# Reordering flips, w transposes and token-mix matmuls in four slots of a retention + phase-MLP kernel

## The chip, the cores and the metric

One core of one Trainium2 chip. The metric is device microseconds of one execution, lower is better. A run is called slow when it is over 1.5% above the fastest run of the same kernel, and fast otherwise.

## The reference, cut to what matters

```python
# retention over q, k, v (4 batches, 8 heads, 768 positions, 64 wide)
state = gamma * state + k_t (x) v_t ;   y_t = scale * q_t @ state
x = y as (4, 768, 512)
# phase MLP
theta = x @ w_theta
zr, zi = x * cos(theta), x * sin(theta)
y = w_tok_r @ zr + w_tok_i @ zi          # mixes the 768 positions
u = x + y
out = u + relu(u @ w_ch)
```

## The kernel before

The retention works in twelve pairs of 128-row blocks, three pairs to a batch. The kernel is scheduled by hand: one slot for each pair, numbered n = 0 to 11 in the code, and called first to twelfth here. In slot n it finishes pair n-1, does most of pair n, prepares pair n+1, loads pair n+3 and mixes some row tiles of the MLP. The order of the calls is the order on every engine. The parts that the change touches:

```python
def prep(n, name, engines):   # cast k, or scale q and v, to bf16 (raw loads are f32)
    ...
def flip(n, name):            # 8 TensorE transposes into a PSUM tile of ring "tr"
    ps = psum.tile([P, 2, NP, P], BF, name="kq_ps", tag="tr", bufs=2)
    ...
    copy(t, ps)               # VectorE, to kqT
def zmul(n, a):               # VectorE: z = (cos, sin) * x
def moe_M(m, lo, hi):         # token mix of row tile m over chunks lo..hi of z; needs wT and z
def moe_u(m):                 # VectorE: u = y + x; frees the PSUM bank of y
def moe_O(m):                 # 4 matmuls u @ w_ch, into ring "tr" too
def moe_out(m):               # VectorE: relu + add; frees that PSUM tile
def w_tok(t0):                # 2 x 6 transposes of w rows, into ring "tr" twice;
                              # copied by VectorE (real) and ScalarE (imaginary)
```

The ring "tr" has two buffers. Every flip, w transpose, transpose of u or of x and output matmul takes the next one in turn and waits until its last reader is done.

In the profile lines below, L183 with kq_ps is a flip, L340 with y_ps a token mix (M), L368 with o_ps an output matmul (O), L393 with w_ps a w transpose, L312 with th_ps a theta matmul, L208 with at_ps the scores and L231 with yT_ps the retention's Y. kqb is a cast k, q or v, and wtr the real part of the transposed w. PE is TensorE and PEld its weight loads, DVE is VectorE, ACT ScalarE, POOL GpSimd, and SPq the queue that issues the DMAs.

```python
# third slot (n = 2), after the first half's mask
    zmul(1, 0)
    ret_A(2, 1)
    ret_mask(2, 1)
    ret_Y(2, 0); ret_I(2, 0); ret_I(2, 1)
    moe_M(0, 2, 3)
    ret_Y(2, 1)
    ret_out(2, 0, AC.copy)
    zmul(1, 1)
    ret_out(2, 1, DV.tensor_copy)
    w_tok(1)
    prep(3, "k", (PL,))
    moe_M(0, 3, 4)
    flip(3, "k")
    ...
# fourth slot and on (nG = 3): n = 3, 4, 5, ...
        if nxt and n > nG + 1: preps(PP)               # q and v of pair n+1, on GpSimd
        ...                                            # theta of pair n-1
        if nxt and nG + 2 < n + 1 < limit: flip(n + 1, name)
        if n == nG + 1 or ...: moe_M(first, 2, 4)
        ...                                            # state, second half of the scores, Y
        if n < U_DMA: moe_U(done)                      # u transposes, copied by ScalarE
        if n in (nG, nG + 1):
            prep(n + 1, "k", (AC,)); preps(DP); flip(n + 1, "k")
        if n == nG or ...: moe_M(first, 2, 4)
        if n in (nG, nG + 1): flip(n + 1, "q")
        if not two:
            moe_M(first, 4, nT); moe_u(first)
            if n < nG + 3: w_tok(n - nG + 3)
        ...
        for t in done: moe_O(t); moe_out(t)
```

## Time and profile before

| | before |
|---|---|
| timed runs | 175.59, 175.73, 175.74 us |
| profiled run | 174.05 us (span 172.3) |
| TensorE busy | 155.0 us, 90% of the span |
| TensorE waiting between 27 and 75 us | 7.9 us in all the waits |
| end of the last matmul | 169.1 us |

The page's second part shows where TensorE is not full. Each digit is its busy share in one fortieth of the span, in tenths:

```profile
PE   7679887799589689899999999999999999999992
```

From the eighteenth digit on TensorE is full. The loose part is the first 75 us, and the change works there.

### The profile page before, as it was taken

What the parts mean: (1) busy time and instruction counts of PE and PEld (TensorE: products, weight loads), DVE (VectorE), ACT (ScalarE), POOL (GpSimd) and SP (SyncE); (2) the same over time, 40 slices, a digit from 0 to 9 for tenths busy, and PEclk for the clock granted to TensorE, in tenths of its full rate; (3) what the DMA queues carried; (4) which work ended last, traced back from release to release, by engine and by line L of the source; (5) the groups of instructions that cost most, each with busy time, mean ns of one, the idle gap of its engine ahead of it and who ended that gap; (6) DMA issues with size and microseconds to landing.
All of it is one profiled execution on the core that took longest, in us unless ns stands there. A gap on an engine that the chain in (4) does not pass through costs nothing.

```text
span 172.3 us, 4658 instructions
## 1 busy us (share of the span) xinstructions
PE 155.0 (90%) x1949; PEld 88.3 (51%) x1975; DVE 104.5 (61%) x138; ACT 81.1 (47%) x139; POOL 64.7 (38%) x81
## 2 busy tenths in 40 slices
PE   7679887799589689899999999999999999999992
PEld 2345655455355456545565555554555444444471
DVE  2368897896565498796757376581854607433443
ACT  7217376373418749579683763918247070000000
POOL 5384769687557397390452617000000000000000
PEclk9999999999999999999999999999999999999998
DMA  4999999999999999959999999995916252564343
GB/s 136 309 335 321 306 270 324 308 384 301 323 279 270 294 295 338 281 42 228 302 208 302 247 265 193 249 123 103 176 30 194 53 143 70 165 145 122 93 152 122
DMA packets 66789, 37.92 MB, mean 220 GB/s; under 512 B 24144, under 2 KB 61264, under 8 KB 66768
## 3 DMA queue, kind: packets, MB, share of 16 engines
q1 hardware_dynamic: 66624, 37.50, 86.5%
q8 instruction: 15, 0.25, 0.7%
q10 hardware_dynamic: 144, 0.13, 0.2%
q14 instruction: 6, 0.05, 0.1%
HBM read 25.69 MB, written 6.29 MB: 186 GB/s over the span
## 4 chain that ended last, share of the span: by engine, by line
PE 79%; DVE 9%; issue 3%; DMA 3%; ACT 2%; POOL 1%; DVEq 0%; SPq 0%; POOLq 0%
PE y_ps L340 33%; PE th_ps L312 12%; PE o_ps L368 12%; PE kq_ps L183 4%; PE at_ps L208 4%; PE yT_ps L231 3%; DMA pair<-in_q_dram 3%; PE st_ps L262 3%; DVE at L215 3%; PE yT_ps L245 3%; DVE kqT L187 2%; PE y_ps L419 2%; DVE xT L285 1%; DVE wtr L400 1%; DVE z L322 1%
## 5 line engine op out<-in xcount | busy, mean ns | idle before, releaser
L340 PE MATMUL y_ps<-z,wtr 128*128 128x512 bf16 x130 | 49.3, 379 | 0.8 <-DVE u L347 0.2
L340 PE MATMUL y_ps<-z,wti 128*128 128x512 bf16 x125 | 47.4, 379 | 0.7 <-issue 0.5
L175 POOL TENSOR_TENSOR kqb<-pair,qscp 128x512 bf16<-128x512 f32 x18 | 19.9, 1122 | 35.2 <-DMA pair<-in_q_dram 27.9
L215 DVE TENSOR_TENSOR at<-at_ps,maskp 128x1024 bf16<-128x1024 f32 x24 | 29.2, 1218 | 6.1 <-PE at_ps L208 6.1
L347 DVE TENSOR_TENSOR u<-y_ps,x_sb 128x512 bf16<-128x512 f32 x23 | 15.8, 690 | 26.2 <-PE y_ps L340 26.2
L175 POOL TENSOR_TENSOR kqb<-pair,vscp 128x512 bf16<-128x512 f32 x24 | 26.2, 1113 | 4.3 <-DMA pair<-in_v_dram 3.5
L285 ACT CAST xT<-yT_ps 128x512 bf16<-128x512 f32 x20 | 13.5, 738 | 26.8 <-PE yT_ps L231 26.8
L368 PE MATMUL o_ps<-wch,uT 128*128 128x512 bf16 x92 | 22.6, 379 | 1.8 <-DVE wtr L400 1.7
L375 DVE SCALAR_TENSOR_TENSOR ot<-o_ps,u 128x512 f32<-128x512 f32 x23 | 15.8, 688 | 13.1 <-PE o_ps L368 13.1
L312 PE MATMUL th_ps<-wth,xT 128*128 128x512 bf16 x93 | 23.0, 379 | 0.2
L322 DVE TENSOR_TENSOR z<-cs,x_sb 128x1024 bf16<-128x1024 bf16 x24 | 19.5, 843 | 2.7 <-DMA x_sb<-xT 2.6
L276 ACT CAST stbd<-st_ps 64x256 bf16<-64x256 f32 x40 | 14.7, 367 | 13.6 <-PE st_ps L262 12.7
L340 PEld LDWEIGHTS <-wtr 128*128 128x128 bf16 x138 | 13.5, 98 | 13.8
L315 ACT ACTIVATE cs<-th_ps,halfpi 128x512 bf16<-128x512 f32 x24 | 16.5, 688 | 8.3 <-PE th_ps L312 7.9
L340 PEld LDWEIGHTS <-wti 128*128 128x128 bf16 x138 | 13.5, 98 | 13.4 <-ACT wti L400 0.5
L316 ACT ACTIVATE cs<-th_ps,zerob 128x512 bf16<-128x512 f32 x24 | 16.5, 686 | 0.0
L183 PE MATMUL kq_ps<-ident,kqb 128*128 128x128 bf16 x136 | 10.3, 219 | 5.9 <-ACT kqb L169 4.4
L368 PEld LDWEIGHTS <-uT 128*128 128x128 bf16 x92 | 8.9, 98 | 11.9 <-issue 2.1
L187 DVE COPY kqT<-kq_ps 128x1024 bf16<-128x1024 bf16 x16 | 10.8, 688 | 6.4 <-PE kq_ps L183 6.2
L312 PEld LDWEIGHTS <-xT 128*128 128x128 bf16 x96 | 9.0, 98 | 10.6 <-DVE xT L285 0.6
L183 PEld LDWEIGHTS <-kqb 128*128 128x128 bf16 x136 | 8.4, 98 | 10.2 <-ACT kqb L169 5.2
L431 ACT COPY uT<-u_ps 128x256 bf16<-128x256 bf16 x2 | 0.7, 372 | 25.5 <-PE u_ps L430 25.5
(61 smaller groups left out, 167.4 us busy)
## 6 DMA issues: line engine op xcount, KB each, us to landing
pair<-in_k_dram SPq DMA_DIRECT2D x12, 512.0 KB, 6.9
pair<-in_q_dram SPq DMA_DIRECT2D x12, 512.0 KB, 7.8
pair<-in_v_dram SPq DMA_DIRECT2D x12, 512.0 KB, 8.2
out_dram<-ot SPq DMA_DIRECT2D x23, 256.0 KB, 2.4
wtok<-in_moe_w_tok_r_dram SPq DMA_DIRECT2D x6, 384.0 KB, 6.6
wtok<-in_moe_w_tok_i_dram SPq DMA_DIRECT2D x6, 384.0 KB, 6.0
w<-in_moe_w_theta_dram SPq DMA_DIRECT2D x1, 1024.0 KB, 8.1
w<-in_moe_w_ch_dram SPq DMA_DIRECT2D x1, 1024.0 KB, 7.4
```

Source lines behind the costliest of these rows:

```text
L175: engines[two].tensor_mul(dst[:, two], src[:, two], _bcast_last(sc[:, 2 * g + two], D))
L183: nc.tensor.transpose(ps[:, two, j, :], st[n, name][:, two, j * P:(j + 1) * P], ident)
L215: nc.vector.tensor_mul(at.rearrange("p a j t -> p (a j) t"), at_ps.rearrange("p a j t -> p (a j) t"), _bcast_mid(maskp[:, two].rearrange(" ...
L285: copy(st[n, "xT"][:, a].rearrange("e j (i w) -> e j w i", w=2), st[n, "y"][a].rearrange("e j (w i) -> e j w i", w=2))
L312: nc.tensor.matmul(th_ps, st[n, "xT"][:, a, j, :], wth[:, j, :], start=(j == 0), stop=(j == NP - 1))
L315: nc.scalar.activation(cs[:, 0, :], th_ps, AF.Sin, bias=halfpi, scale=1.0)
L316: nc.scalar.activation(cs[:, 1, :], th_ps, AF.Sin, bias=zerob, scale=1.0)
L322: nc.vector.tensor_mul(zs[b][:, c], st[n, "cs", a], _bcast_mid(xs[b][:, c, :], 2))
L340: nc.tensor.matmul(y_ps, wT[r][:, s0, t0 * P:(t0 + 1) * P], zs[b][:, s0, r, :], start=(s0 == 0 and r == 0), stop=(s0 == nT - 1 and r == 1))
L347: nc.vector.tensor_add(u, mo[m]["y"], xs[b][:, t0, :])
L368: nc.tensor.matmul(o_ps, mo[m]["uT"][:, j, :], wch[:, j, :], start=(j == 0), stop=(j == nD - 1))
L375: nc.vector.scalar_tensor_tensor(ot, mo[m]["o"], 0.0, mo[m]["u"], ALU.max, ALU.add)
```

## The change

The intent: in the fourth and fifth slot TensorE stands before the flip of a k that has not come, with other matmuls ready behind it. The change puts the work in the order in which its data arrive. In the sixth slot it only moves the w transposes. In the third slot it puts z behind the second mask.

```diff
     state_out(2, 0)
-    zmul(1, 0)
     ret_A(2, 1)
     ret_mask(2, 1)
+    zmul(1, 0)
     ret_Y(2, 0)
     ret_I(2, 0)
     ret_I(2, 1)
-    moe_M(0, 2, 3)
     ret_Y(2, 1)
     ret_out(2, 0, AC.copy)
+    ret_out(2, 1, DV.tensor_copy)
     zmul(1, 1)
-    ret_out(2, 1, DV.tensor_copy)
     w_tok(1)
+    moe_M(0, 2, 3)
     prep(3, "k", (PL,))
     moe_M(0, 3, 4)
+    theta(2, 0)
     flip(3, "k")
     prep(3, "q", DP)
-    theta(2, 0)
     theta(2, 1)
 ... (the slots of the loop)
-        if nxt and n > nG + 1:
+        if n == nG + 1:
+            prep(n + 1, "k", (PL,))
+        if nxt and n > nG:
             preps(PP)
 ...
-            if nxt and nG + 2 < n + 1 < limit:
+            if nxt and nG + 1 < n + 1 < limit:
                 flip(n + 1, name)
-        if n == nG + 1 or n + 1 >= K_DMA and not two:
+        if n + 1 >= K_DMA and not two:
             moe_M(first, 2, 4)
 ...
-        if n in (nG, nG + 1):
+        if n == nG:
             prep(n + 1, "k", (AC,))
             preps(DP)
-            flip(n + 1, "k")
-        if n == nG or n + 1 < K_DMA and n > nG + 1:
+        if n == nG or n + 1 < K_DMA and not two:
             moe_M(first, 2, 4)
-        if n in (nG, nG + 1):
-            flip(n + 1, "q")
+        if n < nG + 3:
+            w_tok(n - nG + 3)
         if not two:
             moe_M(first, 4, nT)
             moe_u(first)
-            if n < nG + 3:
-                w_tok(n - nG + 3)
 ...
-        for t in done:
+        for i, t in enumerate(done):
+            if n == nG:
+                flip(n + 1, "kq"[i])
             moe_O(t)
             moe_out(t)
```

## The prediction

> **What bounds the kernel now.** I read the page first, then TensorE's waits, then the timelines of TensorE, VectorE and GpSimd, then the busy time of the stretches.
>
> ```profile
> PE 155.0 (90%) x1949; PEld 88.3 (51%) x1975; DVE 104.5 (61%) x138; ACT 81.1 (47%) x139; POOL 64.7 (38%) x81
> ...
> PE 79%; DVE 9%; issue 3%; DMA 3%; ACT 2%; POOL 1%; DVEq 0%; SPq 0%; POOLq 0%
> ```
>
> TensorE is the bound: 90% of the span and 79% of the chain that ended last. No TensorE work is removed by the change, so only its idle time can shrink. The waits of TensorE alone between 27 and 75 us (total, times, longest):
>
> ```profile
> PE kq_ps L183 <- ACT kqb L169: 3.7, 2, 2.0
> PE o_ps L368 <- DVE wtr L400: 1.7, 3, 0.6
> PE yT_ps L231 <- DVE at L215: 0.8, 1, 0.8
> PE at_ps L208 <- DVE at L215: 0.7, 1, 0.7
> PE kq_ps L183 <- DVE wtr L400: 0.3, 1, 0.3
> ```
>
> These are what the change aims at: the flip of k waits for ScalarE's cast of k, the output matmul waits for the PSUM buffer that a w transpose used last. The fourth line stays. The ceiling of the gain is 3.7+1.7+0.8+0.3 = 6.5 us. TensorE's timeline shows where (start, length, idle before it in brackets):
>
> ```profile
> 42.74 0.62 PE L359 MATMUL u_ps<-ident,u 128*128 128x128 bf16 x8
> 45.41 0.62 PE L183 MATMUL kq_ps<-ident,kqb 128*128 128x128 bf16 x8 [2.05 <-ACT kqb L169]
> ...
> 49.45 1.89 PE L368 MATMUL o_ps<-wch,uT 128*128 128x512 bf16 x8 [0.58 <-DVE wtr L400]
> ...
> 59.52 1.07 PE L183 MATMUL kq_ps<-ident,kqb 128*128 128x128 bf16 x16 [1.68 <-ACT kqb L169]
> ...
> 62.70 1.02 PE L368 MATMUL o_ps<-wch,uT 128*128 128x512 bf16 x4 [0.58 <-DVE wtr L400]
> ...
> 73.20 1.02 PE L368 MATMUL o_ps<-wch,uT 128*128 128x512 bf16 x4 [0.58 <-DVE wtr L400]
> ```
>
> Slots, by the timeline: third pair 27.1 to 38.6, fourth to 51.2, fifth to 63.6, sixth to 74.1, seventh to 81.8. Stretches (length, then busy us of PE, PEld, DVE, ACT, POOL, clock, DMA share, GB/s):
>
> ```profile
> 38.60:51.20 12.60, 9.73 (x133) 5.86 (x134) 7.78 (x11) 4.29 (x6) 8.69 (x8) 1.00 1.10 308
> 51.20:63.60 12.40, 9.93 (x168) 6.59 (x169) 7.74 (x11) 8.15 (x14) 7.81 (x9) 1.00 1.03 280
> 63.60:74.10 10.50, 9.71 (x168) 6.63 (x169) 8.77 (x11) 7.50 (x14) 6.92 (x7) 1.00 1.01 286
> 74.10:81.80 7.70, 7.49 (x119) 4.17 (x120) 5.87 (x7) 6.29 (x11) 3.43 (x3) 1.00 0.84 144
> ```
>
> So the fourth and fifth slots have 2.9 and 2.5 us of idle TensorE, the sixth 0.8, the rest next to none. But the DMA engines are full (share above 1.0) until 74 us, so loads won't come earlier than now.
>
> **What the Trainium skill says.** "PSUM — Partial Sum Buffer", section "Engine vs sequencer instructions": the queues of ScalarE, VectorE and GpSimd are strictly first in, first out, and matmuls keep program order. The trace agrees: TensorE stood 2.05 us before the flip of k although the matmuls behind it (L340) were ready. So order alone decides which wait is paid. "TensorE: Matmul & The Clock Gate", section "Wait — 56ns, not 53.3ns?": 215.7 ns from start to start at 512 columns, 55.6 at 128. The trace agrees: the chain gives 1.73 us for eight theta matmuls, 0.45 for eight transposes. "SBUF — State Buffer", section "SBUF: two separate sides": a VectorE operation with two SBUF inputs and a GpSimd operation that reads SBUF lock each other out. The trace agrees in kind: z took 0.67 us alone and 1.15 at 28.68, while GpSimd cast w. "DMA: Bandwidth & Descriptors", section "Two DMAs through the same engine are not ordered": descriptors of one queue start in order. I use that for the transposing DMA below; this trace shows only that landings follow issue.
>
> **The change part by part.** Units from the trace: 8 transposes 0.44 us, 12 w transposes 0.67, 4 M or O matmuls 0.86; VectorE copies of kqT 0.6 and wtr 0.55, u and ot 0.69, mask 1.2; ScalarE cast of k 1.05, uT 1.0, wti 0.8; GpSimd k 1.04, q or v 2.04 for both halves.
>
> Third slot (z behind the mask, M and theta moved). VectorE is the bound of this stretch:
>
> ```profile
> 28.68 1.15 DVE L322 TENSOR_TENSOR z<-cs,x_sb 128x1024 bf16<-128x1024 bf16 x1
> 29.76 1.21 DVE L215 TENSOR_TENSOR at<-at_ps,maskp 128x1024 bf16<-128x1024 f32 x1
> 30.89 0.94 DVE L322 TENSOR_TENSOR z<-cs,x_sb 128x1024 bf16<-128x1024 bf16 x1
> 31.75 0.73 DVE L285 CAST xT<-yT_ps 128x512 bf16<-128x512 f32 x1
> 32.38 0.54 DVE L400 COPY wtr<-w_ps 128x768 bf16<-128x768 bf16 x1
> ```
>
> The second mask can start at 29.25, when its scores are there (first mask ends 28.77, scores 0.4), instead of 29.76: Y comes 0.5 earlier. But VectorE idles that half microsecond, and both z follow; the second z now ends near 32.9 instead of 31.83, and M of its chunk waits for it where the flip of k waited for wtr (32.97). Only theta goes before the flip. I work out 0.3 to 0.6 us later at the slot's end. This costs little, since the next slot waits for k and q anyway.
>
> Fourth slot. After the u transposes (end 43.2 now, 43.7 after): M 0.86, w 0.67, M 0.86 fill the hole: 46.2. By then k is cast (ScalarE: uT from 43.9, k from 44.9 to 45.95) and wtr copied (VectorE: q from 44.7 to 45.4, wtr to 45.95). Flip k to 46.7, O to 47.6, flip q to 48.1, then O waits 0.3 for the PSUM buffer that ot frees at 48.4, and ends at 49.25. Now it ends at 51.17: gain 1.9 (2.05+0.58 less 0.3 less the late start and small rests).
>
> Fifth slot. TensorE reaches the flip of k, now behind theta, 4.3 us after the slot's start (today 51.17 to 55.5): 53.55. GpSimd casts k when it lands (issued 43.48, 7.0 to landing: 50.5; ready 51.6), so no wait there. q lands at 52.0 (issued 44.0, 8.0 to landing); both halves are now on GpSimd: 52.1 to 54.15. Flip q wants to start at 54.0: a new wait of 0.2, at most 0.5. w before M frees the buffer of O in time. Gain 1.68+0.58-0.2 = 2.1. The slot ends at about 59.5 instead of 63.56, sum 4.0.
>
> Sixth slot. w before M removes 0.58. Both z now start right at the slot's head and VectorE reaches the copy of x_ps about 0.4 late for the buffer of flip q: gain 0.2, sum 4.2. k cast moved from ScalarE, one q half moved from VectorE and nothing else: no net cost, as neither is full in that stretch.
>
> From there TensorE is dense and everything shifts: 175.73 - 4.2 = 171.5. I add 0.2 for small new waits of the kind I found three of: **171.7**.
>
> **Rivals.** (1) The arrivals win: the stretch to 74 us is bound by DMA, so TensorE gains here and gives it back. For it: DMA share above 1, GpSimd waits 27.9 us in all for q. Against: GpSimd starts q at 60.47 (sixth pair's slot consumes q of the seventh at 68.2 now, 64 after; ready at 62.5) and at 65.85 (ready 67.9, wanted at 73.5). Margins 1.5 and 5 us. Fully true, it would leave about 173.5 to 174.5. (2) The k transpose by DMA of the eighth pair: issued at 74.43, 4.55 us to landing with idle queues; after, issued near 70, behind loads that land until about 74.5, so it lands near 77, wanted at 77.9. The transposed x that follows comes some 1 us late relative to the slot and delays z, ot and the mask, which have about 1.4 us of room. If it fails, 1 us back: 172.7. (3) VectorE becomes the bound of the third slot or of the sixth, because the masks and copies queue behind z: up to 1 us, 172.7. (4) None of the new waits appears: 5.5 us gained, 170.3.
>
> **Range and chances.** Centre 171.7; the low end is rival 4, the high end rivals 2 and 3 together in part: 170.4 to 173.3. The 2% line is at 172.2, only 0.5 above the centre, and a miss of one wait of half a microsecond decides it: faster 0.66, within 2% 0.33. Slower by 2% would need a wait of over 7 us, which nothing shows: 0.01.
>
> **What would show it.** Right: no wait of kq_ps for ScalarE's kqb left after the first slots, no wait of o_ps for wtr; the slots of the fourth, fifth and sixth pair 10.2, 10.3 and 10.3 us long; small waits for kqb from GpSimd near 54, and for ot near 48.3; the third slot's second z ending near 32.9. Wrong: a wait of TensorE over 0.7 us for GpSimd's q near 54, for kqT by DMA near 77, or a longer third slot than by 0.6 us; or wait-free slots whose gain returns behind 75 us.

## The result, and the profile after

The changed kernel took 170.44 us (median of 4 runs, 169.48 to 170.63) against 175.66 us (4 runs, 174.53 to 175.74). The ratio is 0.9706, 95% interval 0.9652 to 0.976: faster. A ratio here is the mean time of one kernel's fast runs over that of the other's fast runs of the same rounds, so it is not quite the ratio of the medians quoted.

The page of the changed kernel: busy shares, the busy tenths, and the chain by engine (the chain is the work that ended last, followed back from the last instruction; shares of the span):

```profile
PE 156.2 (93%) x1949; PEld 89.3 (53%) x1975; DVE 103.0 (61%) x137; ACT 80.2 (48%) x138; POOL 64.7 (38%) x83
...
PE   7969897598999999999999999999999999999991
...
PE 73%; DVE 9%; SPq 7%; DMA 5%; issue 2%; POOL 1%; DVEq 0%
```

TensorE is full from the eleventh digit on. Its weakest digit before the end, the 5 in the eighth place, is the third slot. The chain now also holds DMA and its issue (SPq), which stood at 3% and 0% before: in this trace the load of the third pair's k (8.36 us from 13.43) has become part of what sets the end.

TensorE's waits between 27 and 75 us, the longest first (line waited for, total us, times, longest):

```profile
PE y_ps L340 <- DVE z L322: 1.7, 2, 1.5
PE at_ps L208 <- DVE at L215: 0.6, 1, 0.6
PE yT_ps L231 <- DVE at L215: 0.5, 1, 0.5
PE st_ps L262 <- POOL kqb L175: 0.3, 1, 0.3
```

Both waits that the change aimed at (3.7 us for ScalarE's cast of k, 1.7 us for wtr) are gone. One new wait has come, for z. The waits left out are of 0.2 us each; shorter ones are not listed. TensorE's timeline shows where (start, length, idle before it in brackets):

```profile
33.39 0.38 PE L340 MATMUL y_ps<-z,wtr 128*128 128x512 bf16 x1 [1.48 <-DVE z L322]
...
47.07 0.61 PE L183 MATMUL kq_ps<-ident,kqb 128*128 128x128 bf16 x8
47.52 1.04 PE L368 MATMUL o_ps<-wch,uT 128*128 128x512 bf16 x4
48.61 0.61 PE L183 MATMUL kq_ps<-ident,kqb 128*128 128x128 bf16 x8
49.34 1.02 PE L368 MATMUL o_ps<-wch,uT 128*128 128x512 bf16 x4
...
54.39 1.06 PE L183 MATMUL kq_ps<-ident,kqb 128*128 128x128 bf16 x16
```

The flips of the fourth slot (47.07, 48.61) and of the fifth (54.39) start without a marked wait. The wait of 1.48 us lies in the third slot. Taking the start of each slot's first score matmul from the timelines:

| slot | starts before | starts after | length before | length after |
|---|---|---|---|---|
| fourth | 38.62 | 40.04 | 12.87 | 10.48 |
| fifth | 51.49 | 50.52 | 12.39 | 9.76 |
| sixth | 63.88 | 60.28 | 10.50 | 10.01 |
| seventh | 74.38 | 70.29 | 7.75 | 7.76 |
| eighth | 82.13 | 78.05 | | |

The eighth slot starts 4.08 us earlier, the last matmul ends 4.1 us earlier (165.0), and nothing between gives any of it back. The span shrinks by 3.6 us, because 0.5 us more passes between the last matmul and the last store. The medians differ by 5.2 us. So two things needed experiments: what each slot's part does, with the third slot's loss first, and the 1.1 to 1.6 us between the trace and the medians.

### The profile page after: what moved, and what is told of

The parts are those of the page before. It is cut to its first block, busy times and chain, and to the rows that moved or that the text cites. A ratio compares the mean times of both kernels' runs of the same rounds, so it can differ in the third digit from the quotient of the medians.

```text
span 168.7 us, 4659 instructions
## 1 busy us (share of the span) xinstructions
PE 156.2 (93%) x1949; PEld 89.3 (53%) x1975; DVE 103.0 (61%) x137; ACT 80.2 (48%) x138; POOL 64.7 (38%) x83
## 4 chain that ended last, share of the span: by engine, by line
PE 73%; DVE 9%; SPq 7%; DMA 5%; issue 2%; POOL 1%; DVEq 0%
PE y_ps L340 33%; PE o_ps L368 11%; PE th_ps L312 10%; SPq L81 5%; DMA pair<-in_k_dram 5%; DVE z L322 4%; PE at_ps L208 3%; PE kq_ps L183 3%; PE yT_ps L231 3%; PE st_ps L262 3%; PE yT_ps L245 2%; DVE at L215 2%; PE y_ps L419 2%; PE w_ps L393 1%; SPq L95 1%
## 5 line engine op out<-in xcount | busy, mean ns | idle before, releaser
L340 PE MATMUL y_ps<-z,wtr 128*128 128x512 bf16 x133 | 50.5, 379 | 2.3 <-DVE z L322 1.7
L340 PE MATMUL y_ps<-z,wti 128*128 128x512 bf16 x122 | 46.2, 379 | 0.4 <-issue 0.2
L175 POOL TENSOR_TENSOR kqb<-pair,qscp 128x512 bf16<-128x512 f32 x19 | 20.5, 1092 | 28.4 <-DMA pair<-in_q_dram 17.7
L175 POOL TENSOR_TENSOR kqb<-pair,vscp 128x512 bf16<-128x512 f32 x24 | 25.1, 1066 | 5.2 <-DMA pair<-in_v_dram 5.2
L322 DVE TENSOR_TENSOR z<-cs,x_sb 128x1024 bf16<-128x1024 bf16 x24 | 18.7, 809 | 2.2 <-DMA x_sb<-xT 2.1
L208 PE MATMUL at_ps<-kqT 64*64 64x128 bf16 x384 | 10.6, 221 | 2.2 <-DVE at L215 1.3
L183 PEld LDWEIGHTS <-kqb 128*128 128x128 bf16 x136 | 9.2, 100 | 5.5 <-issue 1.1
```

The lines of the kernel that those rows point to most:

```text
L175: engines[two].tensor_mul(dst[:, two], src[:, two], _bcast_last(sc[:, 2 * g + two], D))
L208: nc.tensor.matmul(at_ps[half, par, j, :], kT[rows, two, j, half], qT[rows, :, j, half], start=(j == 0), stop=(j == NP - 1), skip_group_ch ...
L322: nc.vector.tensor_mul(zs[b][:, c], st[n, "cs", a], _bcast_mid(xs[b][:, c, :], 2))
L340: nc.tensor.matmul(y_ps, wT[r][:, s0, t0 * P:(t0 + 1) * P], zs[b][:, s0, r, :], start=(s0 == 0 and r == 0), stop=(s0 == nT - 1 and r == 1))
```

## The experiments

My theory after the traces: the fourth, fifth and sixth slot each give what their waits were worth, the third slot's part costs 1.4 us, and the usual run of before is longer than its profiled one in some way that the change mends. Rivals: the loads set the pace, so the parts don't add; or the extra of the medians is chance. Runs of one group share a chip and the runs of before (11 of them). Together: e1 to e4, e5 to e8, e9 to e12.

### e1: before again

No edit.

> The kernel before, unchanged, for its trace at its usual time: the profiled run of before took 174.05 us, its timed runs mostly 175.6 to 175.7. Theory: the usual run is longer in the waits that the change removes (the flip of k behind ScalarE's cast, or the arrival of k and q), so a trace near 173.9 us of span shows TensorE idle some 1.5 us more between 42 and 64 us. Rival: the extra time is spread, or lies before 27 us or behind the last matmul, where the change touches nothing. Verdict same: ratio 0.995 to 1.005 under both.

Measured: 174.26 us (174.13 to 174.35 in five runs, one slow run of 177.27 at clock 0.99); ratio 0.9956 (0.9909 to 1.0003). The 11 runs of before beside it fall in two groups: six of 173.96 to 174.41 us at a granted clock of 0.997 to 1.00, five of 175.45 to 176.04 us at 0.988 to 0.990. The trace fell in the first group and showed the old waits unchanged. So the theory, extra waits in the usual run, was wrong: the longer runs have a lower clock. The timed runs on which I built the prediction (175.59 to 175.74) have times of the second group, the trace that I read is of the first.

### e2: without the third slot's part

```diff
 (on the changed kernel: the first hunk of the change undone, the rest kept)
```

> The changed kernel with the third slot as in before (fourth to sixth slot changed). Theory: the third slot's new order costs, since a matmul M now waits 1.48 us for z and the fourth slot starts 1.4 us later (40.04 instead of 38.62 us); ScalarE's copy of uT and cast of k follow that start, so about 1 us of it comes back: 169.3 to 169.7 us against 170.4. Rival: the fourth slot waits for k and q from the DMA anyway, and nothing comes back: 170.2 to 170.6.

Measured: 169.92 us (169.23 to 171.26); ratio 0.9717 (0.9666 to 0.9768). The gain of the third slot was there at first: the fifth slot started at 49.27 us (50.52 with the part) and the eighth at 76.56 (78.05), so 1.2 and 1.5 us; against the second trace of the change (e9, eighth slot at 77.44) it is 0.9 us. Then most of it went back in one wait. The timeline of TensorE, and that of VectorE:

```profile
89.24 0.81 PE L340 MATMUL y_ps<-z,wtr 128*128 128x512 bf16 x2 [1.06 <-DVE u L347]
```

```profile
87.29 1.29 DVE L322 TENSOR_TENSOR z<-cs,x_sb 128x1024 bf16<-128x1024 bf16 x2 [2.97 <-DMA x_sb<-xT]
88.50 0.68 DVE L347 TENSOR_TENSOR u<-y_ps,x_sb 128x512 bf16<-128x512 f32 x1
```

The next token mix needs the PSUM bank of y, which u frees. That u stands on VectorE behind two z, and VectorE stood idle 2.97 us before them for an x that a DMA transposes. In the changed kernel z starts at 87.12, at nearly the same time, though TensorE is 1.5 us later there: the DMA sets this moment, and the changed kernel arrives just late enough not to wait. Both the theory (169.3 to 169.7) and the rival (170.2 to 170.6) missed: 1.5 us came, 1.1 went, but in the ninth slot, by a mechanism that neither named.

### e3: the third slot's part alone

```diff
 (on before: the first hunk of the change alone)
```

> The kernel before with the third slot's new order alone. Theory: the slot ends 1.4 us later and in the fourth slot the cast of k stands behind uT on ScalarE, so nothing absorbs it: 176.5 to 177.2 us. Rival: the wait of 2.05 us for k shrinks by the same amount: 175.5 to 175.9.

Measured: 176.37 us (174.66 to 177.10 in the five fast runs, one slow run); ratio 1.0063 (1.0004 to 1.0122). Its waits between 27 and 75 us show that the fourth slot's wait for k stayed whole, so nothing absorbed a later start:

```profile
PE kq_ps L183 <- ACT kqb L169: 3.7, 2, 2.0
...
PE y_ps L340 <- DVE z L322: 1.0, 1, 1.0
```

This profiled run had clock 0.99, and its trace shows where the clock goes. Stretches (from:to, length, then busy us and counts of PE, PEld, DVE, ACT, POOL, then PEclk, DMA share, GB/s):

```profile
42.50:45.90 3.40, 1.35 (x55) 1.09 (x50) 1.82 (x2) 2.69 (x4) 2.39 (x3) 1.00 0.97 329
45.90:49.40 3.50, 3.28 (x21) 2.13 (x20) 0.90 (x2) 0.00 (x0) 2.32 (x3) 0.51 1.16 302
```

The clock is halved from 45.9 to 49.4 us, right after the hole of 2.05 us before the flip of k. In this trace the third slot's own delay was small: 0.96 us of wait, and the fourth slot starts 0.32 us later than in before. The fourth slot itself is 14.54 us long, 12.87 in before. So most of the 2.0 us by which this trace is behind that of before (span 174.3 against 172.3 us) is the clock and not the order. Five of six runs were at 0.99; the one at 0.996 took 174.66 us, some 0.45 more than before at full clock (174.2, the mean of the six beside it and the five of e1). The median comes near the theory's time, but for another reason, and the size that the theory gave the part (1.4 us) is not confirmed: the fourth slot's start was late by 0.3 here, by 0.9 in e9 and by 1.4 in the first trace of the change, so it varies from run to run. In part this is the moment at which the next k lands: in these three traces the second z ends 0.54 or 0.55 us after GpSimd's cast of k, and that cast ends at 32.24, 32.61 and 32.79.

### e4: the third slot's M behind theta

```diff
 (on the changed kernel)
     w_tok(1)
-    moe_M(0, 2, 3)
     prep(3, "k", (PL,))
-    moe_M(0, 3, 4)
     theta(2, 0)
+    theta(2, 1)
+    moe_M(0, 2, 4)
     flip(3, "k")
     prep(3, "q", DP)
-    theta(2, 1)
```

> The changed kernel, with the two M of the third slot that need z behind both theta and ahead of the flip of k. Theory: theta needs no z, so the wait of 1.48 us for z vanishes and the fourth slot starts about 1 us earlier: 169.2 to 169.8 us. Rival: VectorE is the bound of the third slot, the flip of k or q waits for its copies instead, and the time stays at 170.2 to 170.6.

Measured: 170.31 us (170.08 to 171.54); ratio 0.9748 (0.9696 to 0.9799). The wait for z shrank to 0.2 us and the fourth slot started at 38.82, as the theory had it. The eighth started at 76.60. Then the same wait as in e2, 1.24 us at 89.47, took it back. The time matched the rival, for another reason than the rival's.

### e5, e6, e7: one part alone, on before

```diff
 e5: the fourth slot's new order alone (w ahead of the last M; flip k, O, flip q, O)
 e6: the fifth slot's new order alone (k and q on GpSimd at the head, flips behind theta,
     M later, w ahead of the last M)
 e7: in the fourth, fifth and sixth slot
+        if n < nG + 3:
+            w_tok(n - nG + 3)
         if not two:
             moe_M(first, 4, nT)
             moe_u(first)
-            if n < nG + 3:
-                w_tok(n - nG + 3)
```

> The kernel before with the new order of the fourth slot alone. Theory: TensorE's hole of 2.05 us before the flip of k and the 0.58 us before the output matmuls of that slot go, a rest of 0.1 to 0.3 stays, and nothing later takes it back, as in the trace of the kernel without the third slot's part: 2.2 to 2.4 us less at full clock, about 171.9 us; and since the hole of 2.05 us is gone, no run at a granted clock of 0.99 or less. Rival: the arrivals of the fifth slot's k and q take the gain back: 173 us or more.

> The kernel before with the new order of the fifth slot alone (k of the sixth pair on GpSimd, flips behind theta, w before the last M). Theory: the waits of 1.68 and 0.58 us go, and Y's short wait with them: 2.2 to 2.6 us less at full clock, about 171.8 us; the hole of 2.05 us in the fourth slot stays, so some runs still show a granted clock near 0.99 and take 1.4 us more. Rival: q of the sixth pair, now wholly on GpSimd, is late and costs 0.5 us or more: 172.5.

> The kernel before with nothing but the w transposes ahead of the last M in the fourth, fifth and sixth slot. Theory: each of the three waits of 0.58 us for wtr goes: 1.7 us less at full clock, about 172.5 us. Rival: the same PSUM buffer is then waited for elsewhere (the transposes wait for the copies of kqT just before them): under 1 us less, 173.3 or more.

Measured, e5: 172.04 us (171.84 to 172.28); ratio 0.9833 (0.9793 to 0.9873). Six runs of six at clock 0.997 or more. At full clock before took 174.10 to 174.43 on this chip, and once 175.18, a mean of 174.4: so 2.4 us less. In the trace the fifth slot starts 2.3 us earlier than in before (49.19 against 51.49) and the eighth too (79.84 against 82.13). As the theory had it.

e6: 173.76 us (172.16 to 173.94); ratio 0.991 (0.9858 to 0.9962). Five of six runs were at 0.989 or 0.990; the one at full clock took 172.16, which is 2.2 us less than that mean of before. The fifth slot is 9.77 us long in its trace, 12.39 in before: 2.6 us. GpSimd's q cost no wait. As the theory had it, and the hole left in the fourth slot shows its price again.

e7: 174.66 us (173.60 to 175.25); ratio 0.997 (0.9923 to 1.0017). At full clock 173.60 and 173.77, so 0.7 us less, not 1.7. The theory failed and the rival held. Its waits between 38 and 76 us:

```profile
PE kq_ps L183 <- ACT kqb L169: 3.7, 2, 2.0
PE w_ps L393 <- DVE kqT L187: 0.8, 2, 0.4
```

With the flips left in front, the w transposes take the buffers of the flips, whose VectorE copies are not done: in two slots the wait of 0.58 us for wtr becomes one of about 0.4 us for kqT. In the sixth slot, where the flips come earlier, it goes (9.77 us long instead of 10.50). So in the fourth and fifth slot the w transposes ahead are not enough while the flips stay in front. The flips moved alone were not tried.

### e8: the hole filled with matmuls that nobody reads

```diff
 (on before; the output is unchanged)
         if n < U_DMA:
             moe_U(done)
+        if n == nG:
+            fill = psum.tile([P, dm], FT, name="fill_ps", tag="tr", bufs=2)
+            for _ in range(8):
+                nc.tensor.matmul(fill, warm[:, 0:P], warm, start=True, stop=True)
```

> The kernel before with eight matmuls whose result nobody reads in the hole of 2.05 us of the fourth slot (8 x 0.216 = 1.73 us); the output is unchanged. Theory: the runs of before at a granted clock of 0.988 to 0.990 (5 of 11 on one chip) are those in which the clock is halved for 3.4 us after this hole, as the trace of the third-slot-only kernel shows at 45.96 to 49.37 us; with the hole filled no run has it, and all take the 174.0 to 174.4 us of the full clock. Rival: the halving has nothing to do with the hole; runs at 0.99 and 175.5 us remain in the same share.

Measured: 174.25 us (174.11 to 174.33 in five runs, 176.38 in one at clock 0.99); ratio 0.9977 (0.9924 to 1.003). The wait before the flip fell from 2.05 to 0.3 us. One run in six at the low clock, against four in eleven of before beside it: fewer, but one is not none, so the strict theory fell, and these counts alone don't tell it from the rival. The traces at a low clock help. For each, the 3.4 us ahead of the halving and the 3.4 us of it, first e6:

```profile
42.00:45.40 3.40, 1.45 (x57) 1.18 (x56) 1.44 (x2) 2.65 (x4) 0.42 (x2) 1.00 0.98 263
45.40:48.80 3.40, 3.08 (x19) 2.20 (x21) 1.17 (x2) 0.04 (x1) 3.40 (x4) 0.50 0.98 317
```

Then e7:

```profile
58.20:61.60 3.40, 1.65 (x24) 1.42 (x25) 2.07 (x5) 1.25 (x2) 3.24 (x3) 1.00 0.98 258
61.60:65.00 3.40, 3.18 (x12) 1.50 (x13) 1.41 (x3) 1.74 (x2) 2.49 (x4) 0.50 1.15 333
```

And the later e10:

```profile
27.60:31.00 3.40, 1.95 (x80) 1.59 (x70) 2.76 (x3) 1.20 (x3) 3.40 (x5) 1.00 1.14 336
31.00:34.40 3.40, 3.03 (x28) 1.96 (x19) 2.80 (x4) 1.53 (x2) 1.90 (x2) 0.50 1.14 310
```

The profiled run of e12 has it too, at 30.8 us, with 1.95 us busy ahead. So in all five traces with a halving (e3 included) TensorE was busy for 1.35 to 1.95 of the 3.4 us ahead. There are three such loose stretches: before the fourth slot's flip, before the fifth slot's, and in the third slot. Which of them is hit differs from run to run. But a loose stretch is not enough. The trace of e1 passed the same hole, with as little busy time ahead, at full clock:

```profile
43.56:46.97 3.41, 1.39 (x14) 0.98 (x16) 1.81 (x3) 1.91 (x2) 2.51 (x2) 1.00 1.00 326
```

The record of the clock in the traces shows one thing more. In all fourteen, the changes of the clock that follow its first rise come whole multiples of 3.413 us after it (in e3 12 of them at full clock, then one at half), and this rise comes 4.05 to 7.14 us after the start, at another moment in each run. So the same stretch of the kernel lies differently to these steps in each run. This fits halvings that hit different places, or none; that it decides them is not shown. Over all runs that list a clock: kernels that keep the hole of 2.05 us had 0.990 or less in 29 of 57 runs (before 14 of 33, e1 1, e3 5, e6 5 and e7 4 of 6 each). Kernels without it had it in 6 of 53 (the change 0 of 4 and, in e9, 2 of 6; e2, e4, e5 and e11 0 of 6; e8 and e12 1 of 6; e10 2 of 7). Closing the hole makes the halving rarer; the loose third slot keeps it possible (five of those six runs are of kernels with its new order).

### e9 and e10: the change again, and k of the sixth pair on ScalarE

```diff
 e9: none
 e10 (on the changed kernel)
         if n == nG + 1:
-            prep(n + 1, "k", (PL,))
+            prep(n + 1, "k", (AC,))
```

> The changed kernel, unchanged, beside the three that vary it. 170.2 to 170.6 us, no run at a granted clock below 0.994 under every theory.

> The changed kernel with k of the sixth pair cast on ScalarE at the same place of the program, the head of the fifth slot, instead of GpSimd. Theory: it is the place and not the engine that counts: k lands at 49.9 us, ScalarE has nothing else to do until the theta inputs at 51.2 us, and the time stays within 0.3 us of the changed kernel. Rival: ScalarE, in order, blocks behind a late k and delays xT and theta: 0.5 us or more slower.

Measured, e9: 170.36 us (169.79 to 170.59); ratio 0.9726 (0.9686 to 0.9766). Two of six runs were at 0.986 and 0.987, against what I expected, and cost only 0.3 us there, which is within the spread (170.44 and 170.46, against a mean of 170.14 for the other four, 169.79 to 170.59). This gives the comparison at one clock. Means of the runs at 0.995 or more: before 174.31, the change 170.14, so 4.2 us. The low-clock runs of before beside it average 175.75, 1.4 us more.

e10: 169.90 us (169.16 to 171.56 in the fast runs, one slow run); ratio 0.9693 (0.9644 to 0.9742). The median is 0.46 us below that of the change, more than the theory's 0.3 but away from the rival, and the intervals of the two overlap widely. The traces decide: in e10 the fifth slot is 9.77 us long (52.21 to 61.98), in the change 9.76. ScalarE's timeline in that slot:

```profile
49.25 1.05 ACT L169 CAST kqb<-pair 128x1024 bf16<-128x1024 f32 x1
52.89 1.34 ACT L285 CAST xT<-yT_ps 128x512 bf16<-128x512 f32 x2 [2.59 <-PE yT_ps L231]
```

The cast is done at 50.3, and ScalarE then idles 2.59 us before the next job. So for this k the place counts and not the engine.

That profiled run took 171.56 us for other reasons: the halving at 31.0 us, and a new wait for z in the fourth slot, which is 11.77 us long (10.48 in both traces of the change):

```profile
42.34 0.38 PE L340 MATMUL y_ps<-z,wtr 128*128 128x512 bf16 x1 [1.49 <-DVE z L322]
```

```profile
40.31 1.98 DVE L322 TENSOR_TENSOR z<-cs,x_sb 128x1024 bf16<-128x1024 bf16 x1
```

This z took 1.98 us beside GpSimd's cast of w_ch, which waited for its load and ran from 39.85 to 41.74. In the first trace of the change the same z ended (40.58) just before that cast began (40.67). So 1.5 us can hang on when one load lands.

### e11 and e12: u ahead of z

```diff
 e11 on the kernel of e2, e12 on the kernel of e4; in slots of two tiles
+        if two and n in pairs:
+            moe_u(mine[1])
         if late:
             zmul(n - 1, 0)
             zmul(n - 1, 1)
-        if two and n in pairs:
-            moe_u(mine[1])
```

> The kernel without the third slot's part, with u of the second tile ahead of both z in the slots of two tiles. Theory: there the wait of 1.06 us at 89.2 us was for a u that stood on VectorE behind a z, which waited for the x that a DMA transposes; with u ahead of z the wait goes, and the 1.4 us that the third slot gave stay: 168.7 to 169.3 us. Rival: z itself, or the mask behind it, is what the next slot needs, and the wait only moves: 169.8 to 170.2.

> The kernel with the third slot's M behind theta, with u of the second tile ahead of both z in the slots of two tiles. Theory as for the kernel without the third slot's part: the wait of 1.24 us at 89.5 us goes, 168.8 to 169.4 us. Rival: the wait moves, 170.0 to 170.4.

Measured, e11: 169.15 us (168.95 to 169.52); ratio 0.9666 (0.9627 to 0.9705). All six runs lie below all six of the change on the same chip (169.79 to 170.59), so it beats both kernels. VectorE's timeline:

```profile
86.11 0.69 DVE L347 TENSOR_TENSOR u<-y_ps,x_sb 128x512 bf16<-128x512 f32 x1 [1.99 <-PE y_ps L340]
86.94 1.29 DVE L322 TENSOR_TENSOR z<-cs,x_sb 128x1024 bf16<-128x1024 bf16 x2
```

u now comes at 86.11 instead of 88.50, z as late as before, and TensorE has no wait over 0.2 us left after the third slot. Its last matmul ends at 163.3 us (164.6 in e2). The theory of e2's wait is shown by this.

e12: 169.95 us (168.94 to 171.26); ratio 0.9717 (0.9669 to 0.9766). The wait at 89.5 us is gone from its trace too, but the time sits between the theory and the rival. The profiled run had its clock halved in the third slot. Its other five runs, at full clock, spread from 168.94 to 171.26, and why is not known; a wait like that of e10's fourth slot is a candidate, but none of these five was profiled.

## Why the prediction was right, and where it was not

**Time and class.** Measured 170.44 against 171.7 predicted, at the edge of the range (170.4 to 173.3), and faster by over 2%, as held most likely. The gain at one clock was 4.2 us (e9), as worked out before the 0.2 us added for small waits; the 5.2 us of the medians hold something else besides. That the parts came to 4.2 is partly luck: in the traces the third slot lost 1 us more than worked out, and the fifth and sixth gave 0.8 more.

**The base.** The step that failed was taking 4.2 us, read from a trace of a 174.05 us run, off a median of 175.73 us. The time of that median is the time of runs with a halved-clock stretch (175.45 to 176.04 in e1's group; the fourth timed run, 174.53, came with the result), and the change makes such runs rarer. So I left out about 1 us of gain in the median. The clocks of the first chip's timed runs are not listed, so for that chip this is inferred from the times. The Trainium skill, "TensorE: Matmul & The Clock Gate", section "HAM oscillation — how this bites in real kernels", warns that idle TensorE is re-throttled, but for gaps over about 3.4 us. The longest gap behind the start-up is 2.05 us, and the prediction left the clock out altogether. The runs show halving with that gap.

**Third slot.** Predicted 0.3 to 0.6 us later, measured 1.42 (40.04 against 38.62), more than the 0.6 that the prediction named as a sign of being wrong. The term that was mis-sized is the second z and what hangs on it. VectorE after:

```profile
30.32 1.16 DVE L322 TENSOR_TENSOR z<-cs,x_sb 128x1024 bf16<-128x1024 bf16 x1
31.41 0.72 DVE L285 CAST xT<-yT_ps 128x512 bf16<-128x512 f32 x1
32.02 1.32 DVE L322 TENSOR_TENSOR z<-cs,x_sb 128x1024 bf16<-128x1024 bf16 x1
33.26 0.54 DVE L400 COPY wtr<-w_ps 128x768 bf16<-128x768 bf16 x1
```

It ended at 33.34, not 32.9: it took 1.32 us beside GpSimd's cast of k (31.75 to 32.79), where an end at 32.9 leaves it 0.9. In before it ended at 31.83, just before that cast began (31.86), so the change pushed it into the cast. M of its chunk, which stands ahead of everything else that TensorE had ready, waited 1.48 us for it. Small waits for x_sb, kqT and z followed (0.2 us each). That the loss "costs little, since the next slot waits for k and q anyway" was wrong: k's cast stands behind uT on ScalarE, which follows TensorE, and e2 and e4 show the fifth slot starting 1.2 us earlier without the loss. But e2 also shows that the whole kernel won only 0.4 us at the last matmul by it, because of the ninth slot.

**Fourth slot.** Predicted gain 1.9 with a late start, ending at 49.25; it came 0.97 us ahead of before. The mechanism was right: alone (e5) it gives 2.3. The rest was taken by the third slot's larger delay.

**Fifth slot.** Predicted 2.1, measured 2.6 (also alone, e6). The new wait for q (0.2, at most 0.5) didn't come: TensorE arrived 0.8 us later than reckoned (54.39), and GpSimd was done with q at 53.8. The rest is how idle time is marked. It is counted from the end of the last matmul, 0.38 us after its start with 512 columns and 0.22 with 128, while in full flow the next one starts after 0.22 and 0.06. So a wait costs about 0.16 us more than its mark, here 1.84 and 0.74 us, in sum 2.6. In e7 the removal of a mark of 0.58 made the sixth slot 0.73 us shorter. Moving the cast to GpSimd did no work of its own (e10).

**Sixth slot.** Predicted 0.2, measured 0.5. The removed wait was worth 0.73 (e7) instead of 0.58, and the wait of the flip of q for the copy of x_ps took 0.3 of it (from the start of the flips to the next matmul 1.28 us, 0.98 in before) instead of 0.4.

**Rivals.** Rival 1, the loads win, fell: nothing came back up to the end. Rival 2, the transposing DMA, was right about x and wrong about k: k landed 4.3 us after its issue at 70.22 and cost nothing, while the x that follows became the limit, just not yet in the changed kernel. e2 and e4 ran into it. Rival 3, VectorE bounds the third slot, is what happened, with 1.4 us where I allowed up to 1. Rival 4, no new waits, fell in part: the small wait for q did not come, those for ot (0.3 us, before the O at 49.34) and for x_ps (0.3) did, both too short for a mark above 0.2.

## What to carry to other kernels

When an in-order engine stands before one operation with others ready behind it, move the operation and not only the engine that feeds it; then check which buffer of the ring each moved operation now inherits, since the wait may only change its name (e7). After each gain, look for the next thing on a fixed clock, here a DMA, and for cheap work that stands behind its consumer in a queue (u behind z, e11). And compare trace and median before subtracting one from the other: if they differ by more than the spread, they are different states.

## What the Trainium skill lacked or had wrong

- "TensorE: Matmul & The Clock Gate", section "HAM oscillation — how this bites in real kernels": its rule is no idle gap over about 3.4 us. Here the clock was halved for 3.4 us with no gap over 2.05 us, and in e10 and e12 with none over 0.72 us in the 3.4 us ahead of it; TensorE was busy 1.35 to 1.95 us of the 3.4 us ahead. The page goes on to tell of another kernel, whose short idles between groups of matmuls made its clock change, but gives them no size. The cost in the kernel before was about 1.4 us of 174. What share of busy time is enough stays open: e1 passed with 1.39 us of 3.41, e10 did not with 1.95 of 3.4.
- "SBUF — State Buffer", section "SBUF: two separate sides": it states the lock between VectorE and GpSimd, but not how it looks in a profile, which is a longer VectorE instruction without a marked wait. A two-input product of 128x1024 bf16 took 0.67 us alone and 1.16, 1.32 and (e10) 1.98 us beside GpSimd casts of f32 to bf16, and each of these three ended 0.54 or 0.55 us after its cast (30.94, 32.79 and 41.74).
- No page that I read gives the time to landing of an SBUF transpose by DMA behind loads: that of x took 3.0 us at best and 5.8 us at worst in the trace of before, and that difference decides who waits in the ninth slot.
